# Weight group two: partial words in the attention's PSUM banks, raw words in group three's area

## The chip, the cores and the metric

One core of a Trainium2 chip runs the kernel. The core has a matrix engine (TensorE, PE in the profile), a vector engine (VectorE, DVE), an activation engine (ScalarE, ACT), a general engine (GpSimd, POOL), a queue engine that issues the transfers (SyncE, SP) and 16 DMA engines behind it. SBUF is the on-chip memory that all of them reach; PSUM is a smaller one of eight banks into which TensorE writes, and which VectorE and ScalarE can read and write. The metric is the device time of one execution in microseconds (us), as the median of several runs.

## The reference

Three layers follow each other. The first is a linear attention with a decaying state, the second and third are two-layer networks over 3072 tokens:

```python
state = alpha[:, :, t, :, None] * state + np.einsum('bhd,bhe->bhde', k[:, :, t], v[:, :, t])
y[:, :, t] = np.einsum('bhd,bhde->bhe', q[:, :, t], state)      # 4 x 8 heads, 768 steps, head size 48
h = x @ w_in                                                    # 3072 x 384 by 384 x 2048
g = P / (Q + 1e-06)                                             # P cubic in h, Q = 1 + |b0||h| + |b1|h*h
x = g @ w_out                                                   # 2048 x 384
h = x @ w_in                                                    # 384 x 1024, then a softmax-weighted h,
ln = (solu - mu) / np.sqrt(var + 1e-06) * g_ln                  # a layer norm over 1024, and
return (ln @ w_out).astype(np.float32)                          # 1024 x 384
```

Inputs arrive as 64-bit floats. The kernel reads them as pairs of 32-bit words.

## The kernel before

The sequence is cut into six chunks of 128 steps; a chunk holds 512 tokens (4 batches). Each chunk's attention is done in two halves, 0 to 11 in all; half 2c and half 2c + 1 give the input `xt` of chunk c. The second layer runs over units u = 16c + f, where f counts 16 blocks of 128 of its 2048 inner columns. A unit is `m_up` (nine matmuls into the PSUM tile `hp`, L590, then a chain of ScalarE, VectorE and GpSimd instructions that makes `gh` and `gl`, L595 to L624) and, four units later, `m_down` (nine matmuls into `x2p`, L636). In the program `m_up` of unit u stands behind `m_down` of unit u - 5, and `hp` has three banks.

The weights of the second layer come in four groups of four blocks. `w1_group(n)` makes group n out of seven pieces: three of `w_in` (128 x 512) and four of `w_out` (128 x 384). Each piece goes through `split_w`: a transfer brings the 64-bit words into a staging tile (L531), three integer instructions on VectorE build a 32-bit float out of them (L535, L538, L539; the first two write the partial word `gi` into the tile `fp`, the third writes the float into `ft`), ScalarE rounds it to the high part (L545) and GpSimd subtracts for the low part (L546). Pieces are counted by `stage["n"]`: 0 to 13 are groups zero and one, 14 to 20 group two, 21 to 27 group three; 14 more of the third layer follow later, one at a time (`w2_split`).

Groups zero and one are made ahead of the units, with `stage["wide"]` true and `stage["bank"]` equal to `"x2"`: their `fp` lies in the PSUM banks of `x2p`, and four or five of a group's words go to staging tiles cut out of group two's weight area (`borrow(2, ...)`, the name `lent` in the trace). Group two is made while units 0 to 3 are written into the program, group three while units 4 to 7 are (two pieces' turns per unit, L893 and L897). For both, `fp` is `ft` itself, in SBUF, and all words go through the tile `st`, of which there are two in turn.

The attention's PSUM pool `ps_ap` has two banks (tag `at`), which its tiles take in turn: `a_pe(i)` uses four of them for the scores `sc` (L417, L420), two for `y` (L437, L444), and one for the state update `u` (L477, L483). `a_pe(2)`, the first half of chunk 1, begins in the program at unit 2. Its operands lie in `qks`, a single buffer that is filled by four transfers (L276) out of a copy in HBM (`qk_d`), once per half from half 2 on. Group three's weight area (`lent[3]`, later `g3`) holds the q and k of half 1 in its first third and, behind that, the raw alpha, k and q of half 1 and the raw q of half 0, until PE has turned them.

Each engine's instructions run in the order in which a planner in the tile framework puts them; waits within an engine's list hold all that is behind them. SP issues its transfers in such an order too. `issue_after` pins some instructions of the attention and of `w2_split` behind given units.

Of the kernel before, what the change touches and what calls it, by code (L numbers as in the profile page):

```python
# [7 lines left out]
F32 = mybir.dt.float32  # L8
F32R = mybir.dt.float32r
I32 = mybir.dt.int32  # L10
I64 = mybir.dt.int64
# [12 lines left out]
def _run(*gens):  # L24
    for g in gens:
        for _ in g:
            pass
# [3 lines left out]
def kernel(  # L31
# [23 lines left out]
    NTOK = B * CH  # L55
# [97 lines left out]
    def network(fast):  # L153
# [6 lines left out]
        ps_hp = ps_h.__enter__()  # L160
        if fast:
# [3 lines left out]
            ps_ap = ps_a.__enter__()  # L165
# [18 lines left out]
        def clear():  # L184
            nc.gpsimd.memset(d1, 0.0)
            nc.gpsimd.memset(_view(d1[:], 0, [[PER, NB6 + 1]]), 1.0)
            nc.gpsimd.memset(d2, 0.0)
            nc.vector.memset(alT[:, 0:1], 0.0)
# [3 lines left out]
        def borrow(n, o, dims):  # L192
            if n not in lent:
                lent[n] = moe_pool.tile([128, GW], F32, name=f"lent{n}", tag=f"g{n}")
            size = 1
            for d in dims:
                size *= d
            t = lent[n][:, o:o + size]
            if len(dims) == 1:
                return t  # L200
            nm = "abcd"[:len(dims)]
            return t.rearrange(f"p ({' '.join(nm)}) -> p {' '.join(nm)}", **dict(zip(nm, dims)))
# [139 lines left out]
        def v_load(i):  # L342
            vn = vts[i] = borrow(2, 1024, [B * 256]) if i == 1 else vns
            if i < NPE:
                nc.vector.memset(_view(vn[:], D, [[64, 4 * B], [1, 16]]), 0.0)
            for x in range(2):
                c, b, h = slot(i, 2 * x)
                nc.sync.dma_start(
                    out=vn[:, 512 * x:512 * x + 512].rearrange("p (h d) -> p h d", h=H)[:, :, :D],
                    in_=v[b, :, CH * c:CH * c + CH, :].rearrange("h t d -> t h d"),  # L350
                )
# [153 lines left out]
        stage = {"n": 0, "wide": False, "bank": None}  # L505

        def split_w(src, hi, lo, scale=None):
            keep = None
            if hi is None:
                keep, raw = lo, moe_pool.tile([128, NTOK], I64, name="st", tag="st", bufs=2)  # L510
                n = src.shape[1]
                both = raw[:].bitcast(F32R)
                hi, lo = both[:, :n], both[:, n:2 * n]
            n = src.shape[1]
            x = stage["n"]
            stage["n"] += 1
            ft = moe_pool.tile([128, NTOK], F32, name="ft", tag="ft", bufs=2)
            if stage["bank"] == "x2":
                fp = ps_x2p.tile([128, NTOK], F32, name="fp", tag=f"x2p{x % KT}")
            elif stage["bank"] == "h":  # L520
                fp = ps_hp.tile([128, NTOK], F32, name="fp", tag="h")
            else:
                fp = ft
            if src.dtype == I64:
                if keep is not None:
                    st = raw
                elif stage["wide"] and x % 6 not in (0, 2):
                    st = borrow(2, 2048 + 1024 * (0, 0, 0, 1, 2, 3)[x % 6], [2 * NTOK]).bitcast(I64)
                else:
                    st = moe_pool.tile([128, NTOK], I64, name="st", tag="st", bufs=2)  # L530
                nc.sync.dma_start(out=st[:, :n], in_=src)  # L531
                w32 = st[:, :n].bitcast(I32).rearrange("p (n t) -> p n t", t=2)
                fi = ft[:, :n].bitcast(I32)
                gi = fp[:, :n].bitcast(I32)
                nc.vector.tensor_scalar(  # L535
                    gi, w32[:, :, 1], 3, 0x3FFFFFF8, ALU.logical_shift_left, ALU.bitwise_and
                )
                nc.vector.scalar_tensor_tensor(gi, w32[:, :, 1], -0x40000000, gi, ALU.bitwise_and, ALU.bitwise_or)  # L538
                nc.vector.scalar_tensor_tensor(fi, w32[:, :, 0], 29, gi, ALU.logical_shift_right, ALU.bitwise_or)  # L539
            else:  # L540
                nc.sync.dma_start(out=ft[:, :n], in_=src)
            f = ft[:, :n]
            if scale is not None:
                nc.scalar.activation(f, f, AF.Copy, scale=scale)
            nc.scalar.activation(hi, f, AF.Copy)  # L545
            nc.gpsimd.tensor_tensor(lo, f, hi.bitcast(F32), ALU.subtract)  # L546
            if keep is not None:
                nc.sync.dma_start(out=keep, in_=both[:, :2 * n].bitcast(F32).rearrange("p (x n) -> p x n", x=2))

        def w1_group(n):  # L550
            w = moe_pool.tile([128, GW], F32R, name=f"g{n}", tag=f"g{n}")
            hi, lo = (w[:, 512 * KT * x:512 * KT * (x + 1)].rearrange("p (a b) -> p a b", a=KT) for x in range(2))
            for kt in range(KT):
                split_w(moe_w_in[128 * kt:128 * kt + 128, 512 * n:512 * n + 512], hi[:, kt, :], lo[:, kt, :])
                yield
            wi[n] = (hi, lo)
            hi, lo = (w[:, 4 * DM * x:4 * DM * (x + 1)].rearrange("p (a b) -> p a b", a=4) for x in range(2, 4))
            for f in range(4):
                r0 = 512 * n + 128 * f
                split_w(moe_w_out[r0:r0 + 128, :], hi[:, f, :], lo[:, f, :])  # L560
                yield
            wo[n] = (hi, lo)
# [231 lines left out]
        def take(g, n):  # L794
            for _ in range(n):
                if next(g, "end") == "end":
                    return False
            return True
# [5 lines left out]
        if fast:  # L804
            stage["wide"] = True
            stage["bank"] = "x2"
            pre = w1_group(0)
            _run(a_load(0))
            take(pre, PRE[0])
            v_load(0)  # L810
            consts()
            take(pre, PRE[1])
            _run(a_load(1))
            take(pre, PRE[2])
            v_load(1)
            take(pre, PRE[3])
            nc.gpsimd.memset(Sbd, 0.0)
            _run(a_turn(0), a_pe(0), a_turn(1), a_pe(1), pre)
            clear()
            pre = w1_group(1)  # L820
            take(pre, NA)
            _run(a_load(2, ("ra", "rk")))
            with tc.issue_after(marks[0, 1].ins):
                _run(a_prep(2))
            _run(a_move_qk(2))
            _run(a_enter(2), pre)
            _run(a_load(3, ("ra", "rk")))
            stage["wide"] = False
            stage["bank"] = ""
        else:  # L830
            for n in range(NG):
                _run(w1_group(n))
            x_load(0)
# [39 lines left out]
        for u in range(NU + LAG):  # L873
            c, f = divmod(u, NF1)
            now[0] = u
            if f % (NF1 // 2) == LATE and u < NU:
                _run(side)
                i = 2 * c + 2 + f // (NF1 // 2)
                side = half_steps(i) if fast and i < NH else iter(())
            if u < NU:  # L880
                if f == 0 and c == NCH - 1:
                    if fast:
                        judge(moe_pool)
                    open2()
                    tail = chain(w2_load("i"), n_load(0), w2_load("o"))
                if f == 0 and c and not fast:
                    x_load(c)
                if fast and u < NF1:
                    if f % 4 == 0:
                        _run(prep)  # L890
                        prep = w1_group(f // 4 + 2) if f < 8 else iter(())
                    with later(G1):
                        take(prep, 1)  # L893
                m_up(u)
                if fast and u < NF1:
                    with later(G1):
                        take(prep, 1)  # L897
            if u == NU:
                _run(n_load(1))
            take(side, 1)  # L900
            if u >= U2:
                tp += TP
                with later(G2):
                    take(split2, int(tp))
                tp -= int(tp)
            if tail is not None:
                _run(split2)
                take(tail, 2)
            if u >= LAG:
                m_down(u - LAG)  # L910
            if u - NU + NF1 in EARLY:
                n_tile(EARLY.index(u - NU + NF1))
                if len(EARLY) == B and u - NU + NF1 == EARLY[-1]:
                    n_turn(0)
# [141 lines left out]
```

## Time and profile before

| | |
|---|---|
| median of 3 runs | 798.67 us (797.55 to 798.87) |
| the profiled execution | 796.42 us, of which the span of the trace is 794.7 us |
| VectorE busy | 643.2 us (81% of the span) |
| TensorE busy | 732.0 us (92%) |
| ScalarE, GpSimd busy | 535.5 us (67%), 359.5 us (45%) |
| mean granted TensorE clock | 0.963 of full speed |

Busy time is from an instruction's start to its end in the trace, so time in which an instruction that has started stands still is part of it. A digit of the page's second part is the busy share of one fortieth of the span, 19.9 us, in tenths. The trace's line numbers are those of the kernel before; behind line 526 the changed kernel's are two larger, behind line 890 four.

### The profile page before, as it was taken

Reading aid. Unit: us, or ns where it says so; the run is one execution under the profiler, and the core shown is the slowest. Engines: PE = TensorE matmul, PEld = TensorE weight load, DVE = VectorE, ACT = ScalarE, POOL = GpSimd, SP = SyncE. Lnnn points to the kernel's source line nnn. Section 1 sums busy time; section 2 is a strip of 40 time slices with the busy share of each in tenths; the row PEclk is TensorE's granted clock in tenths of the full one; section 3 lists DMA queues with packets and bytes.
Section 4 is the critical chain, followed back from the end, with each engine's and each line's share of the span. In section 5 each row is a group of like instructions: output and inputs, shape, how many; then the busy total and the mean of one; then the engine's idle time right before and its main releaser. Section 6 shows DMA issues by size and latency. Waiting matters only on the chain.

```text
span 794.7 us, 13903 instructions
## 1 busy us (share of the span) xinstructions
PE 732.0 (92%) x4976; PEld 606.9 (76%) x4976; DVE 643.2 (81%) x1110; ACT 535.5 (67%) x983; POOL 359.5 (45%) x306
## 2 busy tenths in 40 slices
PE   4864986999999989999999999999999999999996
PEld 3753765787777877687777788888888989998996
DVE  5999999979799998979897976567877698777630
ACT  2335756787787868788878879788775555455541
POOL 3256776856555344545454334243242524352322
PEclk9767898999999999999999999999999999999998
DMA  7956466365837275445826160460014443542552
GB/s 172 268 165 187 126 185 134 98 129 164 208 94 179 94 210 143 134 106 162 197 81 160 64 122 15 144 255 0 1 42 106 138 107 100 145 97 60 137 122 69
DMA packets 87279, 101.75 MB, mean 128 GB/s; under 512 B 34464, under 2 KB 63136, under 8 KB 87200
## 3 DMA queue, kind: packets, MB, share of 16 engines
q1 hardware_dynamic: 87104, 100.67, 48.0%
q8 instruction: 41, 0.67, 0.4%
q14 instruction: 38, 0.31, 0.1%
q10 hardware_dynamic: 96, 0.10, 0.0%
HBM read 60.59 MB, written 27.56 MB: 111 GB/s over the span
## 4 chain that ended last, share of the span: by engine, by line
PE 45%; DVE 27%; ACT 7%; DMA 7%; issue 7%; POOL 3%; SPq 3%; DVEq 0%; POOLq 0%; ACTq 0%
PE h L710 13%; PE op L774 12%; PE x2p L636 10%; PE hp L590 9%; DVE ft L539 2%; POOL gl L624 2%; SPq L266 2%; DVE p L616 2%; DVE w L619 2%; DVE alT L324 2%; DVE ft L538 2%; DVE qk L290 2%; DVE p L621 2%; DVE hp L620 2%; DVE ft L535 1%
## 5 line engine op out<-in xcount | busy, mean ns | idle before, releaser
L590 PE MATMUL hp<-xt,g 128*128 128x512 f32 x864 | 226.2, 404 | 16.7 <-DVE p L621 7.7
L590 PEld LDWEIGHTS hp<-xt,g 128*128 128x128 f32 x864 | 163.7, 193 | 59.5 <-DVE p L621 14.2
L624 POOL TENSOR_TENSOR gl<-p,gh 128x512 fp32r<-128x512 f32 x96 | 129.1, 1344 | 175.1 <-ACT gh L623 101.4
L636 PE MATMUL x2p<-gh,g 128*128 128x512 f32 x576 | 196.0, 395 | 0.6 <-ACT gh L623 0.6
L636 PEld LDWEIGHTS x2p<-gh,g 128*128 128x128 f32 x576 | 108.3, 189 | 26.3 <-ACT gh L623 1.4
L636 PE MATMUL x2p<-gl,g 128*128 128x512 f32 x288 | 113.6, 394 | 1.4 <-POOL gl L624 1.4
L774 PE MATMUL op<-w2oh,room 128*128 128x384 f32 x384 | 101.8, 339 | 0.1
L766 POOL TENSOR_TENSOR room<-room,room 128x1024 fp32r<-128x1024 f32 x22 | 53.6, 2438 | 102.2 <-ACT room L765 98.2
L619 DVE SCALAR_TENSOR_TENSOR w<-w,co,hp 128x512 f32<-128x512 f32 x84 | 61.8, 736 | 42.8 <-ACT hp L618 42.4
L710 PE MATMUL h<-w2ih,x 128*128 128x512 f32 x288 | 90.8, 394 | 0.0
L597 ACT ACTIVATE p<-hp,co 128x512 f32<-128x512 f32 x96 | 65.9, 687 | 13.9 <-POOL gl L624 13.4
L618 ACT ACTIVATE hp<-ah 128x512 f32<-128x512 f32 x84 | 50.1, 597 | 32.9 <-DVE p L616 32.2
L616 DVE SCALAR_TENSOR_TENSOR p<-p,co,hp 128x512 f32<-128x512 f32 x84 | 61.7, 734 | 12.7 <-ACT p L597 12.2
L598 ACT ACTIVATE w<-ah,co 128x512 f32<-128x512 f32 x96 | 69.3, 723 | 3.1 <-DVE hp L620 2.9
L774 PEld LDWEIGHTS op<-w2oh,room 128*128 128x128 f32 x384 | 70.0, 188 | 1.7 <-DVE room L766 0.5
L595 ACT ACTIVATE ah<-hp 128x512 f32<-128x512 f32 x96 | 56.7, 590 | 15.9 <-PE hp L590 15.8
L636 PEld LDWEIGHTS x2p<-gl,g 128*128 128x128 f32 x288 | 54.3, 189 | 14.5 <-POOL gl L624 2.6
L623 ACT ACTIVATE gh<-p 128x512 fp32r<-128x512 f32 x96 | 59.9, 624 | 8.1 <-PE x2p L636 3.0
L774 PE MATMUL op<-w2ol,room 128*128 128x384 f32 x192 | 65.0, 339 | 0.0
L621 DVE SCALAR_TENSOR_TENSOR p<-p,co,hp 128x512 f32<-128x512 f32 x84 | 62.2, 740 | 1.2
L710 PEld LDWEIGHTS h<-w2ih,x 128*128 128x128 f32 x288 | 53.9, 188 | 11.7
L617 ACT ACTIVATE ah<-w,co 128x512 f32<-128x512 f32 x84 | 60.6, 722 | 1.3
(168 smaller groups left out, 1281.1 us busy)
## 6 DMA issues: line engine op xcount, KB each, us to landing
room<-room SPq DMA_DIRECT2D x96, 128.0 KB, 2.3
qk_d<-qk SPq DMA_DIRECT2D x10, 771.0 KB, 4.0
st<-in_moe_w_in_dram SPq DMA_DIRECT2D x15, 512.0 KB, 4.9
st<-in_moe_w_out_dram SPq DMA_DIRECT2D x18, 384.0 KB, 4.2
qks<-qk_d SPq DMA_DIRECT2D x20, 257.0 KB, 5.1
x<-x_d SPq DMA_DIRECT2D x18, 256.0 KB, 3.7
out_dram<-o SPq DMA_DIRECT2D x94, 48.0 KB, 1.6
ra<-in_alpha_dram SPq DMA_DIRECT2D x44, 96.0 KB, 2.5
```

Of the source, the lines that this page charges most:

```text
L590: last["PE", u] = nc.tensor.matmul(hp, lhsT=w[:, kt, 128 * o:128 * o + 128], rhs=xts[c][:, kt, xx, :], start=(kt == 0 and w is hi and xx = ...
L597: nc.scalar.activation(p, hp, AF.Square, bias=co[:, 7:8])
L598: nc.scalar.activation(w, ah, AF.Square, bias=co[:, 6:7])
L616: nc.vector.scalar_tensor_tensor(p, p, a1, hp, ALU.add, ALU.mult)
L617: nc.scalar.activation(ah, w, AF.Ln, bias=rest)
L619: nc.vector.scalar_tensor_tensor(w, w, rest, hp, ALU.add, ALU.mult)
L621: fin[u] = nc.vector.scalar_tensor_tensor(p, p, a0, hp, ALU.add, ALU.mult)
L623: last["ACT", u] = nc.scalar.activation(gh, p, AF.Copy)
L624: last["POOL", u] = nc.gpsimd.tensor_tensor(gl, p, gh[:].bitcast(F32), ALU.subtract)
L636: nc.tensor.matmul(x2ps[c][d], lhsT=w[:, o, 128 * d:128 * d + 128], rhs=gg, start=(f == 0 and w is hi and gg is gh), stop=(f == NF1 - 1 an ...
L710: nc.tensor.matmul(hp[:, 512 * n:512 * n + 512], lhsT=x2s[c][:, kt, x, CH * b:CH * b + CH], rhs=w2[w][:, kt, 512 * n:512 * n + 512], start ...
L774: nc.tensor.matmul(op, lhsT=x[:, 128 * f:128 * f + 128], rhs=w2[w][:, f, :], start=(f == 0 and x is hi and w == "oh"), stop=(f == NF2 - 1 ...
```

## The change

While group two is made, `stage["bank"]` is `"at"`: the partial words `fp` of pieces 14 to 20 are tiles of the attention's pool `ps_ap`, and take its two banks in turn with the attention's own tiles. The words of pieces 15, 16, 17 and 19 go to four places in group three's area (at 3072, 4096, 5120 and 2048), those of 14, 18 and 20 to `st` as before. When group two is through, the bank is set to `""`, and group three and the third layer's pieces are made as before. The old branch for a bank `"h"`, which no call set, is gone.

```diff
@@ -517,8 +517,8 @@
             ft = moe_pool.tile([128, NTOK], F32, name="ft", tag="ft", bufs=2)
             if stage["bank"] == "x2":
                 fp = ps_x2p.tile([128, NTOK], F32, name="fp", tag=f"x2p{x % KT}")
-            elif stage["bank"] == "h":
-                fp = ps_hp.tile([128, NTOK], F32, name="fp", tag="h")
+            elif stage["bank"] == "at":
+                fp = ps_ap.tile([128, NTOK], F32, name="fp", tag="at")
             else:
                 fp = ft
             if src.dtype == I64:
@@ -526,6 +526,8 @@
                     st = raw
                 elif stage["wide"] and x % 6 not in (0, 2):
                     st = borrow(2, 2048 + 1024 * (0, 0, 0, 1, 2, 3)[x % 6], [2 * NTOK]).bitcast(I64)
+                elif stage["bank"] and x % 6 not in (0, 2):
+                    st = borrow(3, 2048 + 1024 * (0, 0, 0, 1, 2, 3)[x % 6], [2 * NTOK]).bitcast(I64)
                 else:
                     st = moe_pool.tile([128, NTOK], I64, name="st", tag="st", bufs=2)
                 nc.sync.dma_start(out=st[:, :n], in_=src)
@@ -826,7 +828,7 @@
             _run(a_enter(2), pre)
             _run(a_load(3, ("ra", "rk")))
             stage["wide"] = False
-            stage["bank"] = ""
+            stage["bank"] = "at"
         else:
             for n in range(NG):
                 _run(w1_group(n))
@@ -888,6 +890,8 @@
                 if fast and u < NF1:
                     if f % 4 == 0:
                         _run(prep)
+                        if f:
+                            stage["bank"] = ""
                         prep = w1_group(f // 4 + 2) if f < 8 else iter(())
                     with later(G1):
                         take(prep, 1)
```

The planner's order moves with it. VectorE's list where group two begins, before (`st` is a staging tile of the ring, `hp`, `p`, `w` belong to the units, `Sbd` is the attention's state):

```order
L535 TENSOR_SCALAR ft<-st 128x512
L538 SCALAR_TENSOR_TENSOR ft<-st,ft 128x512
L539 SCALAR_TENSOR_TENSOR ft<-st,ft 128x512
L608 SCALAR_TENSOR_TENSOR hp<-p,co,hp 128x512
L535 TENSOR_SCALAR ft<-st 128x512
L616 SCALAR_TENSOR_TENSOR p<-p,co,hp 128x512
L538 SCALAR_TENSOR_TENSOR ft<-st,ft 128x512
L496 TENSOR_TENSOR Sbd<-u,end 48x8x48 x2
L539 SCALAR_TENSOR_TENSOR ft<-st,ft 128x512
```

and changed (`lent_128` is group three's area):

```order
L537 TENSOR_SCALAR fp<-st 128x512
L540 SCALAR_TENSOR_TENSOR fp<-st,fp 128x512
L610 SCALAR_TENSOR_TENSOR hp<-p,co,hp 128x512
L541 SCALAR_TENSOR_TENSOR ft<-st,fp 128x512
L618 SCALAR_TENSOR_TENSOR p<-p,co,hp 128x512
L496 TENSOR_TENSOR Sbd<-u,end 48x8x48 x2
L537 TENSOR_SCALAR fp<-lent_128 128x512 x2
L540 SCALAR_TENSOR_TENSOR fp<-lent_128,fp 128x512 x2
L615 SCALAR_TENSOR_TENSOR hp<-hp,co,ah 128x512
L541 SCALAR_TENSOR_TENSOR ft<-lent_128,fp 128x512
```

The number and size of the split instructions are the same; their partial words are in `fp`, and pieces 15 and 16 go side by side.

TensorE's list behind the first three units, before (`sc` are the scores of half 2; `g_134` and `g_629` are groups zero and one):

```order
L483 MATMUL u<-lent_175 64x48 x15
L420 MATMUL sc<-qks 128x128 x8
L590 MATMUL hp<-xt,g_134 128x512 x9
L636 MATMUL x2p_1091<-gh,g_134 128x512
L636 MATMUL x2p_1092<-gh,g_134 128x512
L636 MATMUL x2p_1093<-gh,g_134 128x512
L420 MATMUL sc<-qks 128x128 x4
```

and changed, from the same matmuls of `u`, and (behind the mark) from unit 4:

```order
L483 MATMUL u<-lent_175 64x48 x15
L592 MATMUL hp<-xt,g_134 128x512 x9
L638 MATMUL x2p_1094<-gh,g_134 128x512
L638 MATMUL x2p_1095<-gh,g_134 128x512
L638 MATMUL x2p_1096<-gh,g_134 128x512
...
L638 MATMUL x2p_1096<-gl,g_134 128x512
L638 MATMUL x2p_1096<-gh,g_134 128x512
L420 MATMUL sc<-qks 128x128 x4
L592 MATMUL hp<-xt,g_629 128x512 x9
```

The first scores of half 2 stood ahead of unit 3's `m_up`; now they stand behind unit 4's `m_up` and unit 1's `m_down`, and the rest follow one bank at a time, ahead of units 6, 7 and 8. The matmuls of its `y` stood between units 4 and 5 and now stand around unit 8's. Half 3's scores begin ahead of unit 11 in both, its `y` moves from behind unit 12's `m_up` to around those of units 13 and 14, and from unit 19 on the two lists run alike.

SP's list at the end of the first attention loads, before:

```order
L266 DMA rk<-in_k_dram 32x4x192 x4
L652 DMA gln<-in_moe_g_ln_dram 128x8x1
L531 DMA st<-in_moe_w_in_dram 128x512
L531 DMA lent_175<-in_moe_w_in_dram 128x512
L531 DMA lent_175<-in_moe_w_out_dram 128x384
L348 DMA vns<-in_v_dram 128x8x48
```

and changed:

```order
L266 DMA rk<-in_k_dram 32x4x192 x4
L533 DMA lent_128<-in_moe_w_out_dram 128x384 x2
L654 DMA gln<-in_moe_g_ln_dram 128x8x1
L533 DMA st<-in_moe_w_in_dram 128x512
L533 DMA lent_128<-in_moe_w_in_dram 128x512 x2
L533 DMA lent_175<-in_moe_w_in_dram 128x512
L533 DMA lent_175<-in_moe_w_out_dram 128x384
```

The four words of group two that have places of their own are now loaded ahead of most of group one's.

## Rows read from the trace of the kernel before

**Rows 1.** The page's second part: busy tenths of 40 slices.

```profile
DVE  5999999979799998979897976567877698777630
```

**Rows 2.** Windows: length; busy PE, PEld, DVE, ACT, POOL (instructions); clock, DMA share, GB/s.

```profile
66.00:160.00 94.00, 73.28 (x560) 56.13 (x558) 90.66 (x137) 62.76 (x117) 67.80 (x56) 0.89 0.57 150
160.00:500.00 340.00, 325.13 (x2546) 260.50 (x2546) 296.06 (x467) 275.13 (x494) 161.81 (x148) 0.99 0.51 131
```

**Rows 3.** VectorE's windows of L535, L538 and L539 alone, over group two's pieces.

```profile
66.00:107.50 41.50, 5.25 (x7) 0.84 0.57 157
66.00:107.50 41.50, 7.16 (x7) 0.84 0.57 157
66.00:110.40 44.40, 7.50 (x7) 0.85 0.57 156
```

**Rows 4.** Groups by form: count, busy us, mean ns, idle before.

```profile
L539 DVE SCALAR_TENSOR_TENSOR ft<-lent,fp 128x384 int32<-128x384 int32 x6 | 3.2, 534 | 0.0
L538 DVE SCALAR_TENSOR_TENSOR fp<-lent,fp 128x384 int32<-128x384 int32 x6 | 3.1, 549 | 0.0
L535 DVE TENSOR_SCALAR fp<-lent 128x384 int32<-128x384 int32 x6 | 3.1, 547 | 0.0
L535 DVE TENSOR_SCALAR fp<-lent 128x512 int32<-128x512 int32 x3 | 2.1, 700 | 0.4 <-DMA lent<-in_moe_w_in_dram 0.4
L538 DVE SCALAR_TENSOR_TENSOR fp<-lent,fp 128x512 int32<-128x512 int32 x3 | 2.0, 675 | 0.0
L539 DVE SCALAR_TENSOR_TENSOR ft<-lent,fp 128x512 int32<-128x512 int32 x3 | 2.0, 668 | 0.0
```

**Rows 5.** Timeline of VectorE: start us, us, instruction.

```profile
66.04 0.41 DVE L535 TENSOR_SCALAR ft<-st 128x512 int32<-128x512 int32 x1
66.48 2.13 DVE L538 SCALAR_TENSOR_TENSOR ft<-st,ft 128x512 int32<-128x512 int32 x1
...
74.43 0.69 DVE L539 SCALAR_TENSOR_TENSOR ft<-st,ft 128x512 int32<-128x512 int32 x1
...
93.51 0.51 DVE L539 SCALAR_TENSOR_TENSOR ft<-st,ft 128x384 int32<-128x384 int32 x1
...
94.44 0.34 DVE L535 TENSOR_SCALAR ft<-st 128x384 int32<-128x384 int32 x1
```

**Rows 6.** Timeline of GpSimd, one instruction.

```profile
66.27 1.79 POOL L335 TENSOR_TENSOR qk<-qk,P 128x768 f32<-128x768 f32 x1 [1.89 <-DVE qk L290]
```

**Rows 7.** VectorE's waits from 66 to 160 us: total, times, longest.

```profile
DVE ft L535 <- DMA st<-in_moe_w_in_dram: 1.3, 1, 1.3
DVE ft L535 <- DMA st<-in_moe_w_out_dram: 1.3, 1, 1.3
```

**Rows 8.** Timeline of SP's queue: an early load and the refill of `qks`.

```profile
34.29 1.09 SPq L531 DMA_DIRECT2D st<-in_moe_w_in_dram  x1
...
115.14 1.74 SPq L276 DMA_DIRECT2D qks<-qk_d  x4
```

**Rows 9.** Windows again, in the early stretch.

```profile
38.00:42.00 4.00, 2.92 (x44) 2.46 (x44) 4.00 (x11) 2.02 (x4) 1.91 (x2) 1.00 0.91 290
42.00:46.00 4.00, 3.14 (x19) 2.85 (x20) 3.92 (x9) 1.71 (x4) 1.32 (x3) 0.55 0.59 160
```

**Rows 10.** Timeline of TensorE; in brackets the idle time before, and its end.

```profile
79.67 2.04 PE L420 MATMUL sc<-qks 48*128 48x128 f32 x8 [10.56 <-DMA qks<-qk_d]
...
94.77 0.64 PE L444 MATMUL y<-qks,Sbd 128*32 128x128 f32 x16
...
108.96 2.34 PE L590 MATMUL hp<-xt,g 128*128 128x512 f32 x9
...
130.35 1.16 PE L420 MATMUL sc<-qks 48*128 48x128 f32 x16
...
167.48 2.88 PE L590 MATMUL hp<-xt,g 128*128 128x512 f32 x12
```

**Rows 11.** Timeline of VectorE: half 3's `xt`.

```profile
158.77 1.01 DVE L471 TENSOR_TENSOR xt<-y,xt 128x512 fp32r<-128x512 f32 x2
```

## The prediction, made before the changed kernel ran

> **What bounds the kernel now.** I read the shares of busy time first, then windows by stage, then the timelines of VectorE, GpSimd, TensorE and SP where group two is made. Over the whole span TensorE looks like the bound, but the digits of VectorE show another stage in front: from the second slice to the eighth it is at nine tenths or just under [rows 1]. The window from 66 us, where group two's first split instruction starts, to 160 us, shortly before unit 16, says it in numbers: VectorE is busy 90.66 of 94 us, TensorE 73.28, ScalarE 62.76, GpSimd 67.80 [rows 2]. VectorE waits there for little but two transfers of group three's words, 1.3 us each [rows 7]. From 160 to 500 us TensorE is busy 325.13 of 340 us [rows 2], and the planner's lists behind unit 19 are alike in both kernels. So what VectorE saves ahead of 160 us should move all that follows by as much, as long as no other engine takes its place there.
>
> Busy is not the same as working. Piece 14's second instruction starts at 66.48 us and takes 2.13 us [rows 5]; the same form with its partial word in PSUM takes 0.675 us [rows 4]. GpSimd had started an instruction at 66.27 us that ran for 1.79 us, to 68.06 us [rows 6]. From there to the end of VectorE's at 68.61 us are 0.55 us. I read this as an instruction that stands until GpSimd is through and then runs at its own speed. Group two's 21 split instructions show it in sum: 5.25, 7.16 and 7.50 us for L535, L538 and L539, seven each [rows 3].
>
> **The change part by part.** *Partial words in PSUM.* Groups zero and one were split in the form that group two now gets, while GpSimd worked too, and their means are tight: 0.700, 0.675 and 0.668 us for 128 x 512, 0.547, 0.549 and 0.534 us for 128 x 384 [rows 4]. Three pieces of the first size and four of the second make 3 x 2.043 + 4 x 1.630 = 12.65 us, against 5.25 + 7.16 + 7.50 = 19.91 us now. That is -7.3 us on VectorE, which is the path here. The other bound is the case in which GpSimd's instructions have nothing to do with it. Undisturbed, the SBUF form costs 0.41 and 0.34 us for L535 and 0.69 and 0.51 us for L539 [rows 5]; with L538 as in rows 4 that is 3 x 1.775 + 4 x 1.399 = 10.92 us, and the change would cost 12.65 - 10.92 = +1.7 us. I take -7.3: a mean over seven instructions of 1.07 us, where the quickest are half of that, needs a cause, and the starts and ends above give one.
>
> The Trainium skill speaks against the edit: its page "VectorE: DVE Perf Modes", section "Why PSUM operands drop a tier", says that an operand in PSUM bars the mode in which an instruction uses both SBUF read ports. By this rule alone the sum would be the +1.7 us, by the rows -7.3 us. The trace agrees with it for L535, 0.41 us in SBUF and 0.700 us in PSUM.
>
> *Four more staging tiles.* Three of group two's seven pieces now pass through the ring of two `st` tiles instead of seven, so group three's first words can be loaded as soon as piece 18 is through. That can take away VectorE's two waits, 2.6 us together [rows 7], or nothing, since the later pieces of group three still use the ring; I take half, -1.3 us.
>
> *Four loads ahead of group one's.* They are 2 x 0.52 MB and 2 x 0.39 MB, 1.8 MB, put on SP's list ahead of the loads that were issued from 34.29 us on [rows 8]. The DMA engines were busy 0.91 of the time from 38 to 42 us and moved 290 GB/s, and 0.59 from 42 to 46 us [rows 9]. At that rate the 1.8 MB are 6.3 us; VectorE, which is busy 4.00 of 4.00 us there [rows 9], would stand if a piece of group one came later than its turn. Between 0 and +6.3 us I take +1: the share of 0.59 right behind shows room, and most of group one's words are loaded some pieces ahead of their use.
>
> *The attention's banks.* The seven `fp` tiles take turns with the scores of half 2. On VectorE a piece's third instruction frees its bank for the next but one, in the order in which they stand, which costs nothing. Two places cross engines: scores wait for a bank until a piece's third instruction, and piece 20 waits until ScalarE has emptied a bank of scores. Behind the first wait TensorE's whole list is queued, behind the second VectorE's (the next units' chains, the attention's scans). The trace has no such wait. Its nearest is the one of the scores for `qks`, 10.56 us [rows 10]; below it there is no bound but nothing at all, since TensorE is idle 20.7 us of the window [rows 2] and the moved scores take that 10.56 us wait off the units behind them. For VectorE, which is no longer covered by its own lateness and must now wait now and then for a unit's chain through TensorE, ScalarE and GpSimd, I take +1.5 us, nearer to the 1.3 us of its waits in rows 7 than to 10.56. The retired branch and the flag cost nothing: they are settled when the program is built.
>
> *Half 2 gets later.* Its `y` ran at 94.77 us, between units 4 and 5, and is now around unit 8, whose `m_up` was at 108.96 us [rows 10]. `qks` can be filled anew only then. In the old program the refill was issued at 115.14 us [rows 8] and half 3's scores ran at 130.35 us [rows 10]; half 3's `xt` was through at 159.8 us [rows 11] and unit 16 began at 167.48 us [rows 10]. An end of `y` near 112 us is still in time, and behind it lie some 9 us before the scores and 7.7 us before unit 16. I cost it at nothing; where the cover is gone is a rival below.
>
> The sum is -7.3 - 1.3 + 1.0 + 1.5 = -6.1 us. The profiled execution took 796.42 us (its span 794.7 us and 1.7 us around it), so one like it would take 790.3 us. It was 2.25 us quicker than the median, 798.67 us, from which the forecast is made: 792.6 us.
>
> **The rivals.** *New waits take the gain.* VectorE's list stands for banks, transfers and unit chains about as long as it stood for GpSimd: between 2.5 us of gain left and 1.6 us of loss, 796.2 to 800.3 us. For it: TensorE must run 73.28 us in a shorter window and GpSimd 67.80. Against: 14.6 us of idle TensorE would still be left.
>
> *Scores hold TensorE* (the other side). The scores of half 2 stand in TensorE's list ahead of units 5, 6, 7 and 8, each for a bank. TensorE has 20.7 us of idle time in the window, so this decides from 22.3 / 4 = 5.6 us at each place. At 7 us each, two thirds of the wait for `qks`, it is 28 - 20.7 = +7.3 us: 806.0 us. For it: the lists can't overtake, and the planner doesn't know of the time that VectorE stands. Against: pieces 18 and 19, whose banks the first scores need, are through some units earlier in VectorE's list.
>
> *PSUM only costs.* By the skill's rule of the dropped mode VectorE pays and nothing is lifted: +1.7 us, 800.4 us. Worked out from rows 4 and 5, it needs the long instructions in rows 3 to have another cause.
>
> *Nothing happens.* The planner could have kept the instructions in SBUF or undone the order; the lists show `fp` and the new staging tiles, so this is a small case at 798.67 us.
>
> **How the numbers follow.** The forecast has 0.64 (788.8 to 796.2 us: from -7.3 - 2.6 = -9.9 us, where no new wait comes, to a gain of 2.5 us); waits that take it 0.17 (0.08 of it faster, 0.09 the same); scores that hold TensorE 0.12; PSUM that only costs 0.05; nothing 0.02. A measurement of this kernel can tell about 0.2%, 1.6 us. Faster by more than that: 0.64 + 0.08 = 0.72; the same: 0.09 + 0.02 = 0.11; slower: 0.12 + 0.05 = 0.17. The range goes from just under the forecast's lower end, 788.5 us, to 799.0 us in the middle of the case in which waits take the gain; the two slower cases and the rest of that one are left out.
>
> **What would show it.** In the changed profile the 21 split instructions of group two should sum to 12 to 13 us, none over 0.8 us. VectorE's busy time from 66 us to unit 16 should fall by about 7 us, and unit 16 should begin near 161.5 us instead of 167.5 us; from there on the two traces should run in step to the end. Waits of L537 for transfers should be under 2.6 us in sum. The forecast is wrong if VectorE stands idle at piece 20 or at the units' first instructions for several us, if TensorE's row of `sc` has waits beyond 5 us for VectorE, or if VectorE stands between 38 and 60 us for group one's words.

## The result, and the profile of the changed kernel

The changed kernel takes 789.20 us (median of 4 runs, 787.55 to 794.18) against 798.57 us beside it: ratio 0.9891, 95% interval 0.9855 to 0.9926. The prediction was 792.6 us in a range of 788.5 to 799.0 us, faster with a chance of 0.72. The profiled execution took 790.14 us (span 788.4 us), 6.3 us less than the profiled one of before; the working had said 6.1 us less. A repetition beside other kernels gave 787.93 us and a ratio of 0.9867 (0.9851 to 0.9882).

The page's digits of VectorE, which answer to [rows 1], have six nines behind the seventh slice instead of ten:

```profile
DVE  5999999888898889899897966468887788867630
```

The windows of [rows 2] again, and below them the stretch from group two's first split instruction to the end of half 3's `xt`, in the changed kernel and then in the kernel before (length; busy PE, PEld, DVE, ACT, POOL with instructions; clock, DMA share, GB/s):

```profile
66.00:160.00 94.00, 80.07 (x620) 63.23 (x621) 90.39 (x149) 71.79 (x131) 72.64 (x62) 0.93 0.57 148
160.00:500.00 340.00, 326.21 (x2546) 262.01 (x2545) 290.59 (x462) 272.54 (x490) 160.86 (x144) 0.98 0.49 128
...
66.50:151.48 84.98, 71.55 (x556) 56.32 (x557) 84.41 (x139) 64.36 (x118) 66.07 (x56) 0.92 0.55 143
...
66.04:159.78 93.74, 73.02 (x559) 56.11 (x558) 90.40 (x137) 62.72 (x117) 67.64 (x56) 0.89 0.57 150
```

In the same 94 us VectorE is as busy as before and gets 149 instructions done instead of 137, TensorE 620 matmuls instead of 560. The same work (137 and 139 instructions of VectorE) fits into 84.98 us instead of 93.74: VectorE's busy time there is 6.0 us shorter, and its idle time 0.57 us instead of 3.34. TensorE's granted clock in the two stretches was 0.92 and 0.89 of full speed, but the whole 8.8 us stand in VectorE's busy and idle time.

VectorE's windows of L537, L540 and L541 over group two's 21 split instructions answer to [rows 3]: 4.29 + 4.31 + 4.20 = 12.80 us instead of 19.91.

```profile
66.30:99.10 32.80, 4.29 (x7) 0.84 0.51 127
66.30:99.30 33.00, 4.31 (x7) 0.84 0.51 126
66.30:99.30 33.00, 4.20 (x7) 0.84 0.51 126
```

VectorE's timeline at piece 14, beside [rows 5]: the second instruction, 2.13 us before, takes 0.69 us.

```profile
66.50 0.69 DVE L537 TENSOR_SCALAR fp<-st 128x512 int32<-128x512 int32 x1 [0.43 <-ACT lent L396]
67.22 0.69 DVE L540 SCALAR_TENSOR_TENSOR fp<-st,fp 128x512 int32<-128x512 int32 x1
...
68.49 0.68 DVE L541 SCALAR_TENSOR_TENSOR ft<-st,fp 128x512 int32<-128x512 int32 x1
```

TensorE's timeline at unit 3 and unit 16, beside [rows 10]:

```profile
76.79 4.12 PE L592 MATMUL hp<-xt,g 128*128 128x512 f32 x9 [9.14 <-DVE p L616]
...
157.27 2.20 PE L592 MATMUL hp<-xt,g 128*128 128x512 f32 x9
```

The 10.56 us for `qks` are gone, but at the same place TensorE stands 9.14 us for VectorE's last instruction of unit 0 (L616). Unit 3 begins 7.3 us earlier (76.79 instead of 84.08 us), unit 16 10.2 us earlier (157.27 instead of 167.48 us).

### The profile page after: what moved, and what is told of

The parts are those of the page before. It is cut to its first block, busy times and chain, and to the rows that moved or that the text cites. A ratio compares the mean times of both kernels' runs of the same rounds, so it can differ in the third digit from the quotient of the medians.

```text
span 788.4 us, 13907 instructions
## 1 busy us (share of the span) xinstructions
PE 732.6 (93%) x4976; PEld 610.5 (77%) x4976; DVE 634.0 (80%) x1110; ACT 536.4 (68%) x983; POOL 361.9 (46%) x306
## 4 chain that ended last, share of the span: by engine, by line
DVE 37%; PE 30%; ACT 10%; DMA 8%; issue 6%; SPq 5%; POOL 2%; DVEq 0%; ACTq 0%; POOLq 0%
PE hp L592 12%; PE x2p L638 11%; DVE room L752 3%; DVE room L735 3%; SPq L762 2%; PE op L776 2%; ACT jk L737 2%; DVE sm L731 2%; DVE ft L541 2%; DVE room L750 2%; DMA lent<-in_moe_w_in_dram 2%; DMA rq<-in_q_dram 2%; DMA room<-room 2%; DVE p L623 2%; DVE w L621 2%
## 5 line engine op out<-in xcount | busy, mean ns | idle before, releaser
L626 POOL TENSOR_TENSOR gl<-p,gh 128x512 fp32r<-128x512 f32 x96 | 134.4, 1400 | 177.2 <-ACT gh L625 109.3
L592 PEld LDWEIGHTS hp<-xt,g 128*128 128x128 f32 x864 | 163.6, 192 | 57.7 <-DVE p L623 11.6
L776 PE MATMUL op<-w2oh,room 128*128 128x384 f32 x384 | 103.1, 343 | 1.6 <-ACT room L767 1.0
L776 PEld LDWEIGHTS op<-w2oh,room 128*128 128x128 f32 x384 | 71.1, 190 | 3.2 <-ACT room L767 1.3
L776 PE MATMUL op<-w2ol,room 128*128 128x384 f32 x192 | 65.6, 341 | 0.0
```

The lines of the kernel that those rows point to most:

```text
L592: last["PE", u] = nc.tensor.matmul(hp, lhsT=w[:, kt, 128 * o:128 * o + 128], rhs=xts[c][:, kt, xx, :], start=(kt == 0 and w is hi and xx = ...
L626: last["POOL", u] = nc.gpsimd.tensor_tensor(gl, p, gh[:].bitcast(F32), ALU.subtract)
L776: nc.tensor.matmul(op, lhsT=x[:, 128 * f:128 * f + 128], rhs=w2[w][:, f, :], start=(f == 0 and x is hi and w == "oh"), stop=(f == NF2 - 1 ...
```

## The experiments

The ratios are to the kernel before, run beside each kernel. The first question is what the gain is made of. Theory A is that of the prediction: VectorE's instructions with two SBUF operands stand while GpSimd works. Theory B says that the new order on TensorE does it, theory C the staging places.

**One half of the change each.** `staging_only` drops the branch that puts `fp` in PSUM, `bank_only` the branch with the new staging places:

```diff
-            elif stage["bank"] == "at":
-                fp = ps_ap.tile([128, NTOK], F32, name="fp", tag="at")
```

> Half of the change: the words of pieces 15, 16, 17 and 19 go to the four places in group three's area, and the partial words stay in SBUF as in the kernel before. Theory A (VectorE's split instructions with both operands in SBUF stand while GpSimd works, PSUM partial words lift that): group two's 21 split instructions still sum to 18 to 20 us, and only the two waits of 1.3 us for transfers can go, so 796 to 798.6 us, 797.3 as the middle. Theory B (the new order on TensorE gives the gain, as half 2's scores no longer stand ahead of unit 3's matmuls waiting for qks): the scores stand ahead of unit 3 here as before, so 798 to 799 us. Theory C (the staging places give the gain): 789 to 791 us.

```diff
-                elif stage["bank"] and x % 6 not in (0, 2):
-                    st = borrow(3, 2048 + 1024 * (0, 0, 0, 1, 2, 3)[x % 6], [2 * NTOK]).bitcast(I64)
```

> The other half: the partial words of group two go to the attention's two PSUM banks, all its words go through the staging ring as before. Theory A: the 21 split instructions sum to 12.5 to 13 us, VectorE still waits some 1 to 3 us for words, so 790 to 792 us. Theory B: half 2's scores stand behind unit 4 as in the changed kernel, so 789 to 791 us too. Theory C: 797 to 799 us.

`staging_only` has a ratio of 0.9994 (0.9976 to 1.0012), `bank_only` 0.9948 (0.9932 to 0.9964), 793.78 us. The staging places alone bring nothing that can be measured, and theory C falls. One expectation was missed there: group two's 21 split instructions sum to 4.18 + 6.53 + 6.14 = 16.85 us in its profile, not to 18 to 20, though their form is that of before. How long the same instructions stand differs between two orders of the list, and these 3 us less did not shorten the kernel. But the PSUM half alone brings only half of the gain, less than theory A and theory B said. Its 21 split instructions are down to 12.94 us. Two things in its profile go against the gain. First, VectorE reaches the words earlier and waits for them longer than the 2.6 us of [rows 7]:

```profile
DVE fp L537 <- DMA st<-in_moe_w_out_dram: 2.9, 1, 2.9
DVE fp L537 <- DMA st<-in_moe_w_in_dram: 1.6, 1, 1.6
```

Second, group three's split instructions, still in SBUF, stand longer. The windows of L537, L540 and L541 over both groups in `bank_only` give 33.42 us; less group two's 12.94 that is 20.48 us, against 16.86 us before (36.77 over both groups, less 19.91):

```profile
66.40:146.40 80.00, 8.97 (x14) 0.89 0.61 162
66.40:146.40 80.00, 13.01 (x14) 0.89 0.61 162
66.40:146.40 80.00, 11.44 (x14) 0.89 0.61 162
```

So the staging places are worth some 5 us (793.78 us against the changed kernel's 789.20 and 787.93), but only behind a quicker VectorE.

**The same banks and order, one operand moved.** In `one_in_psum` the first instruction writes into `ft` in SBUF, the second reads that and writes `fp`, the third reads `fp`; the banks are held nearly as long, and the order is that of the changed kernel but for a few rows:

```diff
-                gi = fp[:, :n].bitcast(I32)
+                gi = fp[:, :n].bitcast(I32); g0 = fi if stage["bank"] == "at" else gi
                 nc.vector.tensor_scalar(
-                    gi, w32[:, :, 1], 3, 0x3FFFFFF8, ...
+                    g0, w32[:, :, 1], 3, 0x3FFFFFF8, ...
-                nc.vector.scalar_tensor_tensor(gi, w32[:, :, 1], -0x40000000, gi, ...)
+                nc.vector.scalar_tensor_tensor(gi, w32[:, :, 1], -0x40000000, g0, ...)
```

> As the changed kernel, but of the three split instructions of a piece of group two the first writes its partial word to ft in SBUF, the second reads that and writes fp in PSUM, the third reads fp. The attention's banks are taken and freed as in the changed kernel, and the order on the engines is that of the changed kernel but for a few rows. Theory A, when what stands is an instruction with two SBUF operands or one in the quick mode: L537 about 5.25 us and L540 about 7.16 us in sum as before, L541 3.7 us, 16.1 us in sum against 12.7, so 3.4 us slower than the changed kernel: 792 to 793.5 us. Theory B and theory C: as the changed kernel, 788.5 to 790 us.

It has 793.52 us, ratio 0.9939 (0.9920 to 0.9957): 4 to 6 us slower than the changed kernel's two measurements. VectorE's windows of L537, L540 and L541, seven each:

```profile
67.20:92.20 25.00, 3.59 (x7) 0.80 0.65 169
67.20:102.20 35.00, 7.38 (x7) 0.85 0.48 125
67.20:106.20 39.00, 4.20 (x7) 0.87 0.44 114
```

The instruction with two SBUF operands is back at 7.38 us (7.16 in [rows 3]); the third, one operand in PSUM, stays at 4.20. L537 stood less than the 5.25 us expected, and the sum is 15.17 us instead of the 16.1 expected. So the split instructions account for 2.4 us of the 4 to 6 (15.17 - 12.80). From group two's first split instruction to the end of half 3's `xt`, VectorE's idle time also grew, to 3.4 us from 0.57; which instruction causes that was not separated. Theory B said that nothing would change here, and falls as the whole cause.

**The split instructions by themselves.** `split_alone` computes none of the layers:

```diff
+    for _ in range(60):
+        nc.gpsimd.tensor_tensor(gt, raw, gt, ALU.add)          # 128 x 768
+    for _ in range(8):
+        sbuf('b')                                              # three split instructions, partial word in SBUF
+    for _ in range(8):
+        last = psum('b')                                       # partial word in PSUM
...
+        nc.vector.tensor_tensor(sm[:, 0:1], sm[:, 1:2], sm[:, 2:3], ALU.add)
+        nc.vector.tensor_scalar(sm[:, 3:4], sm[:, 4:5], 1.0, None, ALU.add)
```

> Not the layers at all (the output is zeros): the three split instructions of a 128 x 512 piece alone, four pieces in the SBUF form and four in the PSUM form while GpSimd is idle, then eight of each while GpSimd runs additions of 128 x 768 one behind another, then 128 x 1 additions with two SBUF operands and with one. Theory A: with GpSimd idle the SBUF form takes 0.41, about 0.68 and 0.69 us, the PSUM form 0.70, 0.68 and 0.67; with GpSimd busy the SBUF form takes 1.5 to 2.3 us for each instruction that needs both ports and the PSUM form stays within 5% of its idle times; the 128 x 1 addition with two SBUF operands takes about 2 us, the one with a single operand under 0.2. Rival (the long instructions have another cause than GpSimd): no form changes by more than 10% when GpSimd is busy.

Groups by form (count, busy us, mean ns): names with `i` ran with GpSimd idle, with `b` beside its additions; `sf` are the SBUF form, `fp` and `pf` the PSUM form.

```profile
L65 DVE SCALAR_TENSOR_TENSOR sfb<-wd,sfb 128x512 int32<-128x512 int32 x8 | 17.1, 2137 | 0.0
L64 DVE SCALAR_TENSOR_TENSOR sfb<-wd,sfb 128x512 int32<-128x512 int32 x8 | 16.7, 2082 | 0.0
L63 DVE TENSOR_SCALAR sfb<-wd 128x512 int32<-128x512 int32 x8 | 12.9, 1616 | 0.0
...
L64 DVE SCALAR_TENSOR_TENSOR fpb<-wd,fpb 128x512 int32<-128x512 int32 x8 | 5.2, 680 | 0.0
L65 DVE SCALAR_TENSOR_TENSOR pfb<-wd,fpb 128x512 int32<-128x512 int32 x8 | 5.2, 674 | 0.0
L63 DVE TENSOR_SCALAR fpb<-wd 128x512 int32<-128x512 int32 x8 | 5.1, 678 | 0.0
L65 DVE SCALAR_TENSOR_TENSOR sfi<-wd,sfi 128x512 int32<-128x512 int32 x4 | 2.6, 678 | 0.0
L64 DVE SCALAR_TENSOR_TENSOR sfi<-wd,sfi 128x512 int32<-128x512 int32 x4 | 2.6, 677 | 0.0
L64 DVE SCALAR_TENSOR_TENSOR fpi<-wd,fpi 128x512 int32<-128x512 int32 x4 | 2.6, 681 | 0.0
```

With GpSimd idle both forms take 0.68 us for the second and third instruction. With GpSimd at work the PSUM form stays at 0.67 to 0.68 and the SBUF form takes 2.08 and 2.14 us. L63 in SBUF, 0.41 us when nothing is in its way, takes 2.02 us when it meets GpSimd (its mean of 1.62 holds both). This shows theory A's cause by itself. It is also what the Trainium skill says on the page "SBUF — State Buffer", section "Who interferes with whom": an instruction of VectorE with two SBUF inputs, or in a mode with two ports, contends with GpSimd (the former with a GpSimd instruction that reads SBUF, as these additions do), and one with at most one SBUF input outside those modes does not. The numbers agree: L64 and L65 in SBUF have two SBUF inputs, L63 in SBUF has the quick form of 0.41 us, and no PSUM form changes.

The 128 x 1 addition does it too. Three rows of VectorE's timeline: with two SBUF operands it takes 1.65 us, with one never more than 0.15. Of the six with two operands, three take 1.65 us and three 0.16: each long one starts just behind a GpSimd addition's start, each short one just ahead of the next.

```profile
83.44 0.15 DVE L99 TENSOR_SCALAR sm<-sm 128x1 f32<-128x1 f32 x1
83.56 1.65 DVE L97 TENSOR_TENSOR sm<-sm 128x1 f32<-128x1 f32 x1
85.14 0.14 DVE L99 TENSOR_SCALAR sm<-sm 128x1 f32<-128x1 f32 x1
```

**Other banks.** `x2_bank` takes the banks of `x2p` in place of the attention's, and half 2's scores stand ahead of unit 3 as before:

```diff
-            stage["bank"] = "at"
+            stage["bank"] = "x2"
```

> The whole change, but with the partial words of group two in the three PSUM banks of x2p, which are free until unit 0's second matmuls, in place of the attention's two. In the program's lists half 2's scores then stand ahead of unit 3's matmuls as in the kernel before. Theory A: the 21 split instructions sum to 12.5 to 13 us; TensorE's second matmuls of unit 0 may wait for piece 20, 0 to 5 us, of which some lies beside VectorE's work; 789 to 793 us. Theory B: the 10.56 us wait for qks ahead of unit 3 is back and with it the time, 797 to 800 us. Theory C: 789 to 791 us.

> The changed kernel once more, beside the next kernel on one chip, since the first measurement's runs lie 6.6 us apart. Theory A: 0.987 to 0.992 of the kernel before, and the spread has two sources outside the change: when the first loads are through (the start of group two moves with it) and which small VectorE instructions stand behind GpSimd in the third layer.

> The kernel with the partial words in the banks of x2p once more, on the same chip as the changed kernel. Its profile has the scores of half 2 ahead of unit 3 and a wait of 10.59 us for qks there, and group two's start some 2 us later than the changed kernel's, which no instruction of the change explains. Theory A (only VectorE's standing counts, the start is chance): within 0.3% of the changed kernel, 0.988 to 0.993 of the kernel before. Theory B in a weaker form (half the gain is the order on TensorE and the attention's banks): 0.993 to 0.996, 3 to 5 us slower than the changed kernel.

`x2_bank` has 793.02 us and 0.9946 (0.9924 to 0.9968); its repetition 793.99 us and 0.9948 (0.9935 to 0.9961), where the changed kernel beside it had 787.93 us. That is 6 us between them, and the expectation "within 0.3%" was wrong: the choice of the bank, and the order that comes with it, matter, though group two's instructions are short in both. Theory B as first put (797 to 800 us) falls here too, but its weaker form, that half the gain is the order on TensorE and the attention's banks, had said 0.993 to 0.996, and that is what came. Theory A's 789 to 793 us was met at its upper end at most. The profiles of the repetitions are 4.5 us apart in span (791.3 and 786.8). Some 1.0 us of that is there at unit 0 already (58.56 and 57.51 us), where TensorE's lists are still the same. Another part is standing that has only moved. These are VectorE's groups behind 66 us, up to half 3's `xt`, of `x2_again` and then of the changed kernel's repetition:

```profile
L308 DVE TENSOR_TENSOR_SCAN P<-alT,d 128x774 f32<-128x774 f32 x2 | 4.3, 2134 | 0.0
L320 DVE TENSOR_TENSOR qk<-qk,alT 128x768 f32<-128x768 f32 x2 | 3.8, 1892 | 0.0
L317 DVE TENSOR_TENSOR_SCAN alT<-alT,d 128x774 f32<-128x774 f32 x2 | 3.5, 1768 | 0.0
```

```profile
L317 DVE TENSOR_TENSOR_SCAN alT<-alT,d 128x774 f32<-128x774 f32 x2 | 3.9, 1932 | 0.0
L308 DVE TENSOR_TENSOR_SCAN P<-alT,d 128x774 f32<-128x774 f32 x2 | 3.5, 1762 | 0.0
L320 DVE TENSOR_TENSOR qk<-qk,alT 128x768 f32<-128x768 f32 x2 | 1.9, 958 | 0.0
```

The three attention steps, two SBUF operands each, take 11.6 us against 9.3: 2.3 us. Other groups changed both ways, so this is no term of a sum. VectorE's windows from unit 0 to the end of half 3's `xt`, in the same two profiles:

```profile
58.56:157.15 98.59, 95.13 (x155) 0.89 0.49 130
57.51:153.06 95.55, 94.33 (x158) 0.89 0.50 140
```

The stretch is 3.0 us longer with the banks of `x2p`, and 2.2 us of that is idle time of VectorE (3.46 us against 1.22). TensorE's wait for `qks` ahead of unit 3 is there again with 10.93 us; what it adds by itself was not separated.

Taken together, `bank_only`, `one_in_psum` and `x2_bank` each lack one part of the change (the staging places, the first instruction's partial word in PSUM, the attention's banks with the new order on TensorE), and each keeps about half of the gain: 0.9948, 0.9939 and 0.9946. That VectorE's standing is one cause is shown. That it is the only one is not: no run had the new order with all partial words in SBUF.

**Group three too.** `both_groups` keeps the attention's banks until group three is through, its words in the ring:

```diff
-                elif stage["bank"] and x % 6 not in (0, 2):
+                elif stage["bank"] and x < 21 and x % 6 not in (0, 2):
...
-                        if f:
+                        if f > 4:
                             stage["bank"] = ""
```

> The changed kernel, with the partial words of group three (pieces 21 to 27) in the attention's two banks as well; group three's raw words still go through the staging ring. Theory A: group three's 21 split instructions fall from 17.7 us to 12.7, so 4 to 5 us more of gain, 784 to 786 us. Rival: half 3's scores now share the banks with pieces 21 to 27 and get later, and TensorE or VectorE stands for a bank; then it gives back what it saves or more, 789 to 794 us.

784.14 us, ratio 0.9833 (0.9813 to 0.9854); in a repetition 786.10 us, 0.9854 (0.9836 to 0.9871). Windows of L537, L540 and L541 over both groups, 14 pieces:

```profile
67.50:145.50 78.00, 8.49 (x14) 0.91 0.54 146
67.50:145.50 78.00, 8.51 (x14) 0.91 0.54 146
67.50:145.50 78.00, 8.37 (x14) 0.91 0.54 146
```

That is 25.37 us, 12.6 of it group three's, against 17.7 us in the changed kernel (30.49 over both groups). Theory A's number came out. The rival was right that half 3's scores get later: they start at 143.2 us, in the changed kernel beside it at 124.3. But its waits for banks did not come, beyond 0.7 us of the scores for ScalarE; TensorE runs unit 12 first, at 124.0 us instead of 134.6. Here VectorE is busy only 85.00 of the 94 us, and its longest waits are for ScalarE's part of the units:

```profile
66.00:160.00 94.00, 81.85 (x609) 65.65 (x608) 85.00 (x150) 72.40 (x132) 67.67 (x61) 0.93 0.55 150
...
DVE p L618 <- ACT p L599: 3.7, 1, 3.7
DVE hp L615 <- ACT ah L612: 2.0, 1, 2.0
```

**The small instructions of the third layer.** In VectorE's rows the changed kernel keeps a lead of 9.5 to 9.9 us over before down to the tenth step of the third layer, counted from zero, and has 7.56 us from the fourteenth on. The timelines of VectorE and GpSimd at that place (the eleventh step is that of L731's second row):

```profile
638.32 1.21 DVE L731 TENSOR_REDUCE sm<-h 128x1 f32<-128x1024 f32 x1
641.97 2.15 DVE L747 TENSOR_TENSOR sm<-sm 128x1 f32<-128x1 f32 x1 [2.43 <-ACT sm L746]
644.15 0.16 DVE L748 SCALAR_TENSOR_TENSOR sm<-sm 128x1 f32<-128x1 f32 x1
644.34 2.26 DVE L749 SCALAR_TENSOR_TENSOR sm<-sm 128x1 f32<-128x1 f32 x1
...
648.70 1.20 DVE L731 TENSOR_REDUCE sm<-h 128x1 f32<-128x1024 f32 x1
```

```profile
641.69 4.90 POOL L768 TENSOR_TENSOR room<-room,room 128x1024 fp32r<-128x1024 f32 x2 [19.30 <-ACT room L767]
```

Two instructions on 128 numbers each take 2.15 and 2.26 us while GpSimd works. The edit writes them with one tensor and per-partition scalars:

```diff
-            nc.vector.tensor_tensor(t0, r0, r0, ALU.mult)
-            nc.vector.scalar_tensor_tensor(t0, t0, -0.5, ssq, ALU.mult, ALU.mult)
-            nc.vector.scalar_tensor_tensor(r0, t0, 1.5, r0, ALU.add, ALU.mult)
+            nc.vector.tensor_scalar(t0, r0, r0, -0.5, ALU.mult, ALU.mult)
+            nc.vector.tensor_scalar(t0, t0, ssq, 1.5, ALU.mult, ALU.add)
+            nc.vector.tensor_scalar(r0, r0, t0, None, ALU.mult)
```

> The kernel with the partial words of both groups in the attention's banks once more, beside the next two kernels on one chip. Theory A: 0.981 to 0.986 of the kernel before.

> As the kernel with both groups in the attention's banks, and besides the third layer's three 128 x 1 instructions (the Newton step of the layer norm), which now read two SBUF tensors, are written with one tensor and a per-partition scalar operand. In the profiles of before and of the changed kernel these 72 instructions take 28.7 and 29.4 us in sum, where 72 of 0.15 us are 10.8. Theory A (they stand behind GpSimd as the split instructions did, and the 3.7 us that the changed kernel's profile loses at the eleventh step of the third layer is one such case): their sum falls to 11 to 13 us, the loss at that step is gone in every run, and the time falls by 1 to 4 us to 780 to 783 us. Rival (off the path: TensorE sets the third layer's pace, and the loss comes from the transfer of the turned rows): the sum may fall, the time stays within 0.2%.

> The kernel before, with only the third layer's 72 small instructions written with one tensor operand and a per-partition scalar. Theory A: their sum falls from 28.7 to 11 to 13 us; the profile of before does not show the loss at the eleventh step, so 0 to 2 us of gain, 796 to 798 us. Rival (they are off the path): within 0.2% of before.

> The changed kernel, with only the third layer's 72 small instructions written with one tensor operand and a per-partition scalar. The same edit moved the kernel before by nothing (1.0004) and the kernel with both groups in PSUM from 0.983 to 0.985 to 0.979 of the kernel before. Theory A (what the small instructions cost depends on where the third layer stands against GpSimd; the changed kernel's first profile lost 3.7 us at the eleventh step, its second lost nothing there): 0.982 to 0.987 of the kernel before, 784 to 788 us. Rival (only the kernel with both groups has the loss): 0.987 to 0.991, as the changed kernel.

| kernel | without the edit | with it |
|---|---|---|
| before | 798.43 us | 798.54 us, 1.0004 (0.9994 to 1.0014) |
| changed | 0.9867 and 0.9891 | 788.38 us, 0.9879 (0.9861 to 0.9897) |
| both groups | 0.9833 and 0.9854 | 781.32 us, 0.9787 (0.9771 to 0.9804) |

The 72 instructions fall from 28.7 to 14.9 us in sum, 0.21 us each, a little above the 11 to 13 expected. Before and changed kernel gain nothing by it: there the rival holds. With both groups it is 4.8 us against the repetition, which ran beside it, and 2.8 against the first measurement, and this is the fastest kernel of the study. The loss explains part of that: in both profiles of `both_groups` and in the first of the changed kernel the lead falls by about 2 us for good at the eleventh step (in `bank_only` by 1.3), and in the latter TensorE waits 1.0 us for ScalarE and 0.6 us for VectorE ahead of the third layer's output matmuls (L776); in the changed kernel's repetition, in `both_small` and in the two other kernels with the edit the lead does not fall there. The repetition kept its lead without the edit, so the edit is not all that decides it. What the rest of `both_small`'s gain is, stays open.

## Why the prediction was right, point by point

*The bound.* VectorE's lateness ahead of 160 us did set what follows: from unit 16 to the last, 95, the starts of the units lie 7 to 12 us apart in the two traces, and 9.6 us are kept into the third layer. Not every microsecond saved there counts: group two's split instructions took 3 us less in `staging_only`, at the same time for the whole kernel.

*Partial words in PSUM,* -7.3 us: 19.91 - 12.80 = -7.1 us, as forecast. None of the 21 takes over 0.8 us. But this term is not the gain by itself: with the same short instructions `bank_only` and `x2_bank` gained 4 to 5 us. The other bound, in which PSUM only costs, is refuted by `split_alone`.

*Staging tiles,* -1.3 us: mis-sized, and wrong in kind. Both waits went, 2.8 us of idle time. But `staging_only` shows that the places have no worth of their own, and `bank_only` that without them the shorter instructions turn into 4.5 us of waits. The two terms are no sum.

*Loads ahead of group one's,* +1 us: about nothing. Group two starts 0.46 us later, and 0.37 us of that are there at 18 us, where the lists are the same. This start moves by more than that by chance: 66.50 and 67.95 us in the changed kernel's two profiles.

*Banks and new waits,* +1.5 us: mis-sized, 0.4 us up to half 3's `xt`. Scores never held TensorE for a bank. I said that the wait for `qks` would be off the units' way. It is, but TensorE stands nearly as long for VectorE (9.14 us instead of 10.56): the old wait hid VectorE's lateness.

*Half 2 later,* 0: right, with the reason turned round. The refill of `qks` is issued at 113.59 us, 1.6 us earlier than before.

*What the sum left out.* Other instructions with two SBUF operands changed as well: up to half 3's `xt`, L308 takes 5.3 instead of 6.1 us, L317 5.6 instead of 6.6 and L313 0.7 instead of 1.4, together 2.5 us, while group three's split instructions take 0.8 us more. None of these was edited. By theory A, which of them stands depends on where GpSimd's work falls; that was not followed instruction by instruction. So only the first term of such a gain could be forecast here.

*The numbers.* Up to the third layer the gain was larger than forecast (9.6 us against 6.1); the profiled run then lost 2.0 us at the eleventh step and 1.3 us in its last 35 us, which is how 6.3 came out so near: by luck. From the median, 798.6 to 789.2 us, it is 9.4 us, so 789.2 lies nearer to the range's lower end (788.5) than to the forecast of 792.6. It was right to forecast from the median and not from the starting run, which was 2.25 us quicker.

One sentence of the prediction misnames a row: the `m_up` at 108.96 us is unit 7's, not unit 8's, whose row in the trace of before is this:

```profile
116.21 2.37 PE L590 MATMUL hp<-xt,g 128*128 128x512 f32 x9
```

The term for half 2 was argued from it. With unit 8's own row, `y` would have been expected to end near 119 us, behind the old refill at 115.14, and the room in front of half 3's scores would have been smaller. The term came out at nothing because unit 8 itself began 9.0 us earlier, at 107.24 us.

## What to carry to other kernels

Look for one form of a VectorE instruction with very different durations, and lay GpSimd's timeline beside it: where both engines worked, an instruction with one SBUF operand (the other in PSUM, or a per-partition scalar) took less time here than the SBUF form that is quicker alone. Whether the kernel gets faster by it depends on the path: the small instructions of the third layer were halved in three kernels and only one gained. When such an engine gets quicker, give it its inputs earlier in the same edit, since each alone may show half or nothing. A gain from less standing is to be followed into the instructions that were not touched.

## What the runs showed of the hardware

An instruction on 128 x 1 numbers with two SBUF operands stood about as long as one on 128 x 512: it took 1.65 us instead of 0.16 in `split_alone` (2.28 instead of 0.68 for 128 x 512), and up to 2.26 us in the rows of the third layer. GpSimd pays as well: its additions took 2.04 us beside the SBUF form and 1.80 behind VectorE's last instruction, as these groups show (27.3 to 67.5 us, and 90 to 140 us).

```profile
L89 POOL TENSOR_TENSOR gt<-raw,gt 128x768 f32<-128x768 f32 x19 | 38.8, 2044 | 1.5
...
L89 POOL TENSOR_TENSOR gt<-raw,gt 128x768 f32<-128x768 f32 x28 | 50.5, 1802 | 2.2
```

L63 in its quick SBUF form stood in `split_alone` even while GpSimd only filled tiles: its first pair, from 5.06 us, took 4.68 us where a later pair took 0.75, and GpSimd's first fill ran to 8.51 us, a second to 9.47.
